# One place per operation in a planned order: attention and a gated MLP on one core

## The chip, the cores and the metric

The kernel runs on one core of a Trainium2 chip. The metric is the device time of one launch in microseconds. The engines are TensorE (PE, matmuls; its weight loads are listed as PEld), VectorE (DVE), ScalarE (ACT), GpSimd (POOL) and SyncE (SP, which issues most DMAs).

## The reference

```python
# attention: q, k, v of shape (4, 8, 576, 64)
q_rot, k_rot = (rotate(q), rotate(k))            # rotary embedding over halves of 64
scores = scale * np.matmul(q_rot, k_rot.transpose(0, 1, 3, 2))
scores = scores - np.max(scores, axis=-1, keepdims=True)
attn = np.exp(scores)
attn = attn / (np.sum(attn, axis=-1, keepdims=True) + 1e-09)
attn_out = np.matmul(attn, v)
# MLP over x = attn_out as (2304, 512), with w_in (512, 2048) and w_out (2048, 512)
h = x @ w_in
g = h * (1.0 / (1.0 + np.exp(-1.702 * h)))
return g @ w_out
```

## The kernel before, in words

**Tiling.** The 32 heads are worked on as 16 pairs. For a pair, `prep` (with `prep_qk`) loads q, k and v, applies the rotary embedding on POOL or DVE, and turns q and k with TensorE (L463). `scores` (L515) makes five blocks of scores; `softened` reduces each on DVE (L528), applies the exponential on ACT (L531), and for pairs 4 to 15 transposes 32x32 blocks on DVE (L536). `weighted` then forms the value product for pairs 4 to 15 in two halves of many small matmuls (L580); pairs 0 to 3 turn the weights on TensorE (L616) and use `weighted_whole`. `inverse_sums` brings the row sums through DRAM. The result is split into a high and a low part and written to `x_dram`.

**MLP.** Each product with float32 weights is made from such parts. `weight` loads one of 32 weight tiles (L710, into OW), converts it in nine steps on ACT (L714, L716), DVE (L718, L720, L723) and POOL (L726), and writes both parts into `win` or `wout`. `moe` works on chunks of 256 tokens: per block of 128 hidden columns twelve matmuls of the first layer into PT (L759), tanh on ACT (L765), a multiply on DVE that frees PT (L767), a split into G (ACT or POOL, then DVE or POOL), and six matmuls of the second layer (L776). The last four chunks are made by `two_chunks` with seven instead of eight products per pair of blocks; it needs sums of x (`sums`, tiles A and SX), made on DVE, and combinations of the weights (`differences`), which go through `t_dram`.

**What sets the order.** Every operation is given to a planner: `Plan.op` records it with its durations per engine it may run on, its dependences, its buffers, a priority and a release time. `Plan.run` plays the program through once as a list scheduler: whenever an engine is idle, it takes the ready operation with the lowest priority number whose buffers are free. For operations that two engines can do, the choice falls there too. The instructions are then issued in the order of the planned starts, so that each engine's queue has that order and runs it strictly, with waits on semaphores. In the kernel before, the priorities are times: tables for the pairs (PREP_AT, PAIR_AT, PAIR_LEN), the MLP (MOE_AT, MOE_STEP), the weights (WEIGHT_AT; WEIGHT_FROM is the release of their loads) and `differences` (T_AT), offsets in PLANNED, and NUDGE, which shifts 30 single operations.

Of the kernel before, what the change touches and what calls it, by code (L numbers as in the profile page):

```python
# [36 lines left out]
               -26154, 61379, -126384, 132121, -99291, -14531]  # L37
T_AT = [420394, -239827, 396523, 706563, 493117, 510553, 65805, 610849]
MORE_TIMES = ['T_AT']
NUDGE = {80: 7902, 153: 682, 235: 3974, 311: -1562, 313: -665, 315: 5307, 317: 1694, 320: 989, 394: -6842, 890:  # L40
         16599, 1142: -7665, 1171: 1126, 1181: -8648, 1199: -256, 1208: -44, 1252: 9550, 1943: -1091, 1953: 561,
         1955: 10337, 2043: 21717, 2131: 12833, 2217: 1319, 2236: -2623, 2245: -5223, 2316: -13089, 2610: 8963, 2746:
         819, 2970: 2878, 2976: 26303, 2977: 2097}
SLOTS = dict(SPS=3, PT=2, RAW=2, RAW1=1, BT=1, KP=2, ST=2, RT=3, XS=1, XC=4, T=1, G=1, O=2, OW=2, CW=2, TP=1, VR=1)
EARLY = dict(RAW=2, RAW1=1, BT=1, XS=1, KP=2, TP=1, VE=2, OW=3, CW=3)
ATTENTION = ("RAW", "RAW1", "BT", "KP", "ST", "RT", "XS", "TP", "VR")
# [5 lines left out]
PE, ACT, DVE, POOL, SP = "PE", "ACT", "DVE", "POOL", "SP"  # L52
# [25 lines left out]
class Plan:  # L78
# [23 lines left out]

    def op(self, durs, fn, deps=(), bufs=(), prio=0.0, moved=None, chain=None, columns=0.0,
           release=0.0, port=(), mode=("", ""), code=0.0):
        prio = prio + NUDGE.get(len(self.ops), 0.0)
        o = Op(len(self.ops), durs, fn, list(bufs), prio, moved, columns, release, port, mode, code)
        for d in {id(d): d for d in deps if d is not None}.values():
            d.out.append(o)
            o.before += 1
        if chain is not None:  # L110
            if chain in self.chains:
                self.chains[chain].then.append(o)
                o.before += 1
            self.chains[chain] = o
        for b in o.bufs:
            b.users.append(o)
        self.ops.append(o)
        return o
# [172 lines left out]
def attention_moe(ctx: ExitStack, tc: tile.TileContext, q, k, v, w_in, w_out, cos_sin, out):  # L291
# [69 lines left out]
    def dma(fn, nbytes, *deps, full=0, part=0, row=2048, land=900.0, by=SP, **kw):  # L361

        work, n = nbytes * (0.83 / row + 0.0032), full + part
        return op(by, 400.0 * full + 610.0 * part, fn, *deps,
                  moved=(work + 50.0 * n, work / n + 550.0, land + 300.0), **kw)
# [31 lines left out]
    def f():  # L397
        nc.vector.memset(plan.tiles["T"][0], 0.0)

    zeros = op(DVE, 140.0, f, prio=-1e6)  # L400
    warm = plan.buf("PT")
    for i in range(at["n_warm"]):
# [3 lines left out]
    def f():  # L406
        nc.gpsimd.memset(ident, 1.0)
        nc.gpsimd.affine_select(ident, ident, [[-1, 128]], compare_op=ALU.is_equal, fill=0.0, base=0,
                                channel_multiplier=1)

    constants = op(POOL, 1200.0, f, prio=-1e6)
    n_ve = early["VE"]

# [636 lines left out]
```

## Time and profile before

| What | us |
|---|---|
| median of 3 runs (690.1 to 691.67) | 690.37 |
| span of the profiled execution | 686.1 |
| the profiled execution's own total | not given beside the span |
| busy PE / PEld | 650.9 / 521.2 |
| busy DVE / ACT / POOL | 475.7 / 364.3 / 266.0 |

The span runs from the first to the last instruction of one profiled execution; the runs are timed without a profile. Busy times add up what the instructions of an engine cover, with the ends of pipelined matmuls modelled. Windows cut the span into stretches, the timeline shows instructions in order of time with the idle time just before them and what ended it, and the waits add such idle time by who waited for whom.

### The profile page before, as it was taken

The numbers are of one execution on the slowest core, as the hardware profiler recorded it, in microseconds if no ns is written. First come the engines' busy times: TensorE is split into PE (matmuls) and PEld (weight loads), VectorE is DVE, ScalarE is ACT, GpSimd is POOL, SyncE is SP. The second block draws the span as 40 slices with busy tenths as digits, with TensorE's granted clock in tenths as the row PEclk, the third lists the DMA queues.
The fourth block names the chain that finished last, engine by engine and source line by source line (L and its number), as shares of the span: only waits on it lengthen the run. The fifth ranks groups of instructions, "written<-read, shape, count | busy, mean of one in ns | idle before, by whom it ended". The sixth has DMA issues, their size and how long they took to land.

```text
span 686.1 us, 17932 instructions
## 1 busy us (share of the span) xinstructions
PE 650.9 (95%) x7160; PEld 521.2 (76%) x7160; DVE 475.7 (69%) x1041; ACT 364.3 (53%) x896; POOL 266.0 (39%) x269
## 2 busy tenths in 40 slices
PE   6899995999999999899999999999999999999997
PEld 4565554776778677767787878787989899998996
DVE  4999898899799889477847385728268445646342
ACT  2998985657676646254536253525235444533343
POOL 3766746635553567477663243111101000111000
PEclk8999999999999999999999999999999999999999
DMA  7965549668767556582737244143356223342111
GB/s 168 198 175 167 140 138 265 142 176 236 188 178 206 146 151 198 153 312 82 227 119 208 51 113 96 45 132 83 105 195 215 73 113 123 123 169 78 63 62 61
DMA packets 97539, 100.70 MB, mean 147 GB/s; under 512 B 61984, under 2 KB 81712, under 8 KB 93232
## 3 DMA queue, kind: packets, MB, share of 16 engines
q1 hardware_dynamic: 96400, 99.30, 50.0%
q8 instruction: 56, 0.92, 0.5%
q10 hardware_dynamic: 1056, 0.26, 0.2%
q14 instruction: 27, 0.22, 0.1%
HBM read 65.26 MB, written 23.67 MB: 130 GB/s over the span
## 4 chain that ended last, share of the span: by engine, by line
PE 71%; DVE 10%; DMA 8%; issue 4%; ACT 3%; POOL 2%; SPq 2%; POOLq 0%; DVEq 0%; ACTq 0%
PE SPS L941 13%; PE PT L759 13%; PE SPS L776 12%; PE SPS L515 9%; PE SPS L580 7%; PE PT L900 6%; PE SPS L900 6%; DMA OW<-in_moe_w_in_dram 2%; DVE TP L528 2%; DVE TP L536 2%; PE PT L616 2%; DMA OW<-in_moe_w_out_dram 2%; PE PT L463 2%; DMA RAW<-in_k_dram 2%; DMA RAW<-in_q_dram 1%
## 5 line engine op out<-in xcount | busy, mean ns | idle before, releaser
L759 PEld LDWEIGHTS PT<-XC,win 128*128 128x128 f32 x960 | 123.7, 190 | 23.7 <-DVE T L767 8.1
L759 PE MATMUL PT<-XC,win 128*128 128x256 f32 x960 | 134.3, 287 | 7.2 <-DVE T L767 4.5
L776 PE MATMUL SPS<-wout,G 128*128 128x512 f32 x480 | 131.8, 405 | 1.3 <-POOL G L359 1.3
L531 ACT ACTIVATE TP<-TP,ST 128x576 f32<-128x576 f32 x144 | 111.0, 773 | 33.7 <-DVE TP L528 33.1
L528 DVE TENSOR_SCALAR_CACHE_REDUCE TP<-SPS 128x576 f32<-128x576 f32 x144 | 103.8, 750 | 13.3 <-PE SPS L515 12.9
L515 PE MATMUL SPS<-KP 64*128 64x288 f32 (+1 forms) x640 | 103.5, 434 | 3.4 <-DVE TP L528 2.3
L776 PEld LDWEIGHTS SPS<-wout,G 128*128 128x128 f32 x480 | 83.7, 189 | 27.4 <-issue 6.9
L941 PE MATMUL SPS<-wout,G 128*128 128x512 f32 x384 | 93.0, 392 | 0.0
L359 DVE TENSOR_TENSOR G<-T,G 128x256 fp32r<-128x256 f32 x121 | 54.9, 463 | 50.8 <-ACT G L347 45.0
L536 DVE STREAM_TRANSPOSE TP<-TP 128x576 f32<-128x576 f32 x108 | 80.9, 765 | 10.4 <-ACT TP L531 10.0
L941 PEld LDWEIGHTS SPS<-wout,G 128*128 128x128 f32 x384 | 70.4, 188 | 13.9
L515 PEld LDWEIGHTS SPS<-KP 64*128 64x128 f32 (+1 forms) x640 | 54.3, 178 | 32.2 <-DVE TP L528 7.5
L347 ACT CAST G<-T 128x256 fp32r<-128x256 f32 x114 | 44.8, 405 | 63.6 <-PE SPS L776 46.1
L580 PE MATMUL SPS<-TP,VR 32*64 32x160 f32 (+1 forms) x3456 | 67.7, 293 | 9.1 <-issue 5.9
L580 PEld LDWEIGHTS SPS<-TP,VR 32*64 32x64 f32 x3456 | 59.2, 130 | 16.2 <-issue 10.7
L726 POOL TENSOR_TENSOR CW<-CW 128x512 int32<-128x512 int32 x32 | 42.8, 1339 | 62.1 <-DVE CW L723 17.7
L359 POOL TENSOR_TENSOR U<-U,U 128x256 f32<-128x256 f32 x16 | 12.0, 749 | 139.3 <-ACT U L347 109.0
L765 ACT ACTIVATE T<-PT 128x256 f32<-128x256 f32 x80 | 30.5, 381 | 49.9 <-PE PT L759 38.5
L767 DVE SCALAR_TENSOR_TENSOR T<-T,PT 128x256 f32<-128x256 f32 x80 | 33.1, 413 | 27.8 <-ACT T L765 27.2
L359 POOL TENSOR_TENSOR XS<-XS 128x576 fp32r<-128x576 f32 (+1 forms) x24 | 34.1, 1423 | 42.6 <-ACT XS L347 15.8
L350 POOL TENSOR_SCALAR G<-T 128x256 fp32r<-128x256 f32 x30 | 12.9, 428 | 77.5 <-PE SPS L776 37.8
L359 POOL TENSOR_TENSOR BT<-RAW,cos_sin_sb 128x512 f32<-128x512 f32 (+1 forms) x29 | 29.0, 1003 | 33.8 <-DMA RAW<-in_k_dram 12.9
(103 smaller groups left out, 936.9 us busy)
## 6 DMA issues: line engine op xcount, KB each, us to landing
TR<-t_dram SPq DMA_DIRECT2D x16, 1024.0 KB
VR<-VR SPq DMA_DIRECT2D x36, 288.0 KB
x_dram<-XS SPq DMA_DIRECT2D x16, 576.0 KB
XC<-x_dram SPq DMA_DIRECT2D x18, 512.0 KB
OW<-in_moe_w_in_dram SPq DMA_DIRECT2D x16, 512.0 KB
OW<-in_moe_w_out_dram SPq DMA_DIRECT2D x16, 512.0 KB
t_dram<-TS SPq DMA_DIRECT2D x8, 1024.0 KB
out_dram<-O SPq DMA_DIRECT2D x18, 256.0 KB
```

The source lines that it names most:

```text
L347: return nc.scalar.copy(to, src)
L359: return engine[e].tensor_tensor(to, a, b, op=how)
L515: nc.tensor.matmul(ss[h].t[:, c, 0:HALF] if t < 4 else ss[h].t[rows, c, 0:HALF], kq.t[rows, 1, t * 128:t * 128 + (128 if t < 4 else 64)], ...
L528: o = vec("DVE", "psum", S, lambda e: nc.vector.tensor_scalar(tp.t[:, t].rearrange("p (c s) -> p c s", c=2), s.t[:, :, 0:HALF], -1.0, LARG ...
L531: o = vec("ACT", "sbuf", S, lambda e: nc.scalar.activation(tp.t[:, t], tp.t[:, t], AF.Exp, bias=st.t[:, 0, t:t + 1], scale=-1.0, accum_out ...
L536: return o, vec("DVE", "psum", S, lambda e: nc.vector.transpose(tp.t[:, t], tp.t[:, t]), o, bufs=[tp], prio=prio + at["exp"] + at["across"])
L580: nc.tensor.matmul(bank[64 * h:64 * h + 64, to:to + 32 * (s1 - s0)], vr.t[rows, h, a], tp.t[rows, s0:s1, 32 * a:32 * a + 32], start=(a == ...
L726: o = vec("POOL", "two", DM, lambda e, a=a, r=r: nc.gpsimd.tensor_tensor(a().bitcast(I32), a().bitcast(I32), r(), op=ALU.add), o, low, buf ...
L759: nc.tensor.matmul(h.t[:, 0:CT], win[f_i // KH][:, wl, kk, f_i % KH * 128:(f_i % KH + 1) * 128], xc[xl].t[:, kk, :], start=(i == m == 0), ...
L776: nc.tensor.matmul(acc.t[:, m, :], g.t[:, a, m * 128:(m + 1) * 128], wout[f_i // KH][:, b, f_i % KH, :], start=(f_i == fs[0] and i == 0), ...
L900: nc.tensor.matmul(h(to), w(a)[:, k], x(b)[:, k], start=(begin and n == 0), stop=(n == 5), skip_group_check=True)
L941: nc.tensor.matmul(acc[j].t[:, m, :], g.t[:, x, m * 128:(m + 1) * 128], wout[f_i // KH][:, y, f_i % KH, :], start=(begin and n == 0), stop ...
```

## The change

Each operation gets a place of its own, by its number in the order in which the code creates the operations. The place takes the part of the priority; the release comes from HELD where the number stands in it and is 0 elsewhere; a letter in ENGINES would leave an operation one engine only. NUDGE is gone. The tables of times are still in the code, but for each of the 2998 operations the place overrides them. HELD has 16 numbers, all of them loads of weights; ENGINES has 2998 dots. No operation, dependence or buffer is changed.

```diff
-NUDGE = {80: 7902, 153: 682, 235: 3974, 311: -1562, 313: -665, 315: 5307, 317: 1694, 320: 989, 394: -6842, 890:
...
+PLACES = [2, 0, 10, 18, 11, 8, 17, 15, 19, 6, 12, 16, 14, 3, 1, 7, 5, 21, 22, 24, 27, 31, 9, 28, 32, 35, 38, 42, 41,
...
+          2984, 2986, 2988, 2989, 2996, 2997]
+HELD = {1161: 61703, 1170: 33528, 1197: 49667, 1206: 107335, 1215: 94361, 1224: 0, 1251: 58829, 1296: 97830, 1305:
+        101045, 1323: 8666, 1332: 92779, 1341: 156202, 1359: 91161, 1377: 1324, 1395: 60303, 1413: 114354}
+ENGINES = ("...................................................................................................."
...
-        prio = prio + NUDGE.get(len(self.ops), 0.0)
+        n = len(self.ops)
+        if n < len(PLACES):
+            prio, release = PLACES[n], HELD.get(n, 0.0)
+            if ENGINES[n] != ".":
+                e = {"A": ACT, "V": DVE, "G": POOL}[ENGINES[n]]
+                durs = {e: durs[e]}
```

## Rows read from the trace of the kernel before

**Rows 1.** Windows: from:to and length, busy us of each engine, PEclk, DMA, GB/s
```profile
0.00:20.00 20.00, 13.10 (x70) 9.84 (x70) 11.32 (x24) 6.99 (x16) 8.39 (x17) 0.83 0.78 174
20.00:100.00 80.00, 75.29 (x571) 45.65 (x569) 73.87 (x165) 72.98 (x173) 53.11 (x46) 1.00 0.63 167
100.00:124.00 24.00, 16.31 (x349) 11.78 (x348) 19.10 (x39) 12.69 (x33) 12.78 (x10) 0.93 0.70 195
124.00:340.00 216.00, 206.19 (x2790) 162.55 (x2790) 180.73 (x376) 127.00 (x305) 126.14 (x120) 1.00 0.67 189
340.00:500.00 160.00, 158.80 (x2263) 128.59 (x2263) 92.28 (x207) 67.36 (x173) 48.32 (x52) 1.00 0.39 109
500.00:512.00 12.00, 10.75 (x68) 9.37 (x67) 8.05 (x17) 3.92 (x9) 0.00 (x0) 1.00 0.34 126
512.00:676.00 164.00, 164.00 (x1036) 148.55 (x1035) 89.13 (x217) 70.25 (x186) 17.25 (x26) 1.00 0.32 112
676.00:686.10 10.10, 6.47 (x28) 4.90 (x27) 1.25 (x4) 3.10 (x7) 0.00 (x0) 1.00 0.27 104
```

**Rows 2.** Chain that ended last, 478 to 515 us: start, us, what
```profile
496.53 1.43 PE PT L759 x12
...
505.58 3.09 DVE A L359 x5
```

**Rows 3.** Timeline of PE, 100 to 124 us: start, us, instruction, [idle before, releaser]
```profile
108.65 2.73 PE L580 MATMUL SPS<-TP,VR 32*64 32x160 f32 x144 [2.92 <-DVE TP L536]
...
114.34 2.40 PE L580 MATMUL SPS<-TP,VR 32*64 32x128 f32 x118 [2.07 <-issue]
...
120.26 0.58 PE L759 MATMUL PT<-XC,win 128*128 128x256 f32 x2 [2.15 <-issue]
```

**Rows 4.** Timeline of ACT and PE around 150 and 232 us
```profile
149.98 0.70 ACT L714 ACTIVATE CW<-OW 128x512 int32<-128x512 uint32 x1 [2.47 <-DMA OW<-in_moe_w_in_dram]
...
153.57 1.09 PE L759 MATMUL PT<-XC,win 128*128 128x256 f32 x7 [1.26 <-DVE T L767]
...
232.05 0.66 ACT L714 ACTIVATE CW<-OW 128x512 int32<-128x512 uint32 x1 [2.38 <-DMA OW<-in_moe_w_out_dram]
...
233.49 1.22 PE L759 MATMUL PT<-XC,win 128*128 128x256 f32 x8 [1.25 <-DVE T L767]
```

**Rows 5.** Timeline of SP's queue: the loads that ACT waited for in rows 4
```profile
143.68 0.54 SPq L710 DMA_DIRECT2D OW<-in_moe_w_in_dram  x1
...
224.92 1.35 SPq L710 DMA_DIRECT2D OW<-in_moe_w_out_dram  x1
```

**Rows 6.** Waits of ACT for weight loads, whole span: total us, times, longest
```profile
ACT CW L714 <- DMA OW<-in_moe_w_out_dram: 5.9, 4, 2.4
...
ACT CW L714 <- DMA OW<-in_moe_w_in_dram: 4.3, 3, 2.5
```

**Rows 7.** Waits of PE, 124 to 340 us: total us, times, longest
```profile
PE SPS L580 <- issue: 3.5, 5, 1.6
PE PT L759 <- DVE T L767: 2.9, 3, 1.3
PE SPS L776 <- POOL G L359: 1.3, 2, 1.1
PE PT L549 <- ACT KP L354: 0.9, 1, 0.9
```

**Rows 8.** Timeline of PE: second halves of products of pairs 6, 7 and 9
```profile
178.01 1.59 PE L580 MATMUL SPS<-TP,VR 32*64 32x128 f32 x74 [0.91 <-issue]
...
214.95 2.73 PE L580 MATMUL SPS<-TP,VR 32*64 32x160 f32 x144
...
279.69 0.79 PE L580 MATMUL SPS<-TP,VR 32*64 32x128 f32 x28 [1.57 <-issue]
```

**Rows 9.** One line's instructions on DVE (ns min/median/max), and a group of the page
```profile
L718 DVE TENSOR_SCALAR CW<-CW x32: 379/428/1518, 19.0 to 241.5; 128x512 f32<-128x512 f32 x32
...
L528 DVE TENSOR_SCALAR_CACHE_REDUCE TP<-SPS 128x576 f32<-128x576 f32 x144 | 103.8, 750 | 13.3 <-PE SPS L515 12.9
```

More of the change, by code (lines that the diff above doesn't have):

```diff
@@ L39 @@
 MORE_TIMES = ['T_AT']
-NUDGE = {80: 7902, 153: 682, 235: 3974, 311: -1562, 313: -665, 315: 5307, 317: 1694, 320: 989, 394: -6842, 890:
-         16599, 1142: -7665, 1171: 1126, 1181: -8648, 1199: -256, 1208: -44, 1252: 9550, 1943: -1091, 1953: 561,
-         1955: 10337, 2043: 21717, 2131: 12833, 2217: 1319, 2236: -2623, 2245: -5223, 2316: -13089, 2610: 8963, 2746:
-         819, 2970: 2878, 2976: 26303, 2977: 2097}
+PLACES = [2, 0, 10, 18, 11, 8, 17, 15, 19, 6, 12, 16, 14, 3, 1, 7, 5, 21, 22, 24, 27, 31, 9, 28, 32, 35, 38, 42, 41,
[157 rows of a table added]
@@ new lines @@
+HELD = {1161: 61703, 1170: 33528, 1197: 49667, 1206: 107335, 1215: 94361, 1224: 0, 1251: 58829, 1296: 97830, 1305:
+        101045, 1323: 8666, 1332: 92779, 1341: 156202, 1359: 91161, 1377: 1324, 1395: 60303, 1413: 114354}
+ENGINES = ("...................................................................................................."
+           "...................................................................................................."
+           "...................................................................................................."
+           "...................................................................................................."
+           "...................................................................................................."
+           "...................................................................................................."
+           "...................................................................................................."
+           "...................................................................................................."
+           "...................................................................................................."
+           "...................................................................................................."
+           "...................................................................................................."
+           "...................................................................................................."
+           "...................................................................................................."
+           "...................................................................................................."
+           "...................................................................................................."
+           "...................................................................................................."
+           "...................................................................................................."
+           "...................................................................................................."
+           "...................................................................................................."
+           "...................................................................................................."
+           "...................................................................................................."
+           "...................................................................................................."
+           "...................................................................................................."
+           "...................................................................................................."
+           "...................................................................................................."
+           "...................................................................................................."
+           "...................................................................................................."
+           "...................................................................................................."
+           "...................................................................................................."
+           "..................................................................................................")
```

156 rows, old and new, of the table PLACES are left out of this document.

## The prediction, made before the changed kernel had run

> **What bounds the kernel now.** I read the windows first, then what TensorE waits for, then the timeline around the largest gaps, then the chain of waits. The windows [rows 1] show TensorE (PE) as the bound: it is busy 650.91 of 686.10 us, so 35.19 us are idle, and these lie in this way: 0 to 20 us 6.90; 20 to 100, where only attention runs, 4.71; 100 to 124, 7.69; 124 to 340, where attention and the MLP are mixed and the late weights come in, 9.81; 340 to 500, 1.20; 500 to 512, at the change to the last four chunks, 1.25; 512 to 676 nothing; the tail 3.63. VectorE (DVE) is close behind PE until 340 us (73.87 of 80 us, then 180.73 of 216) and has room after that (92.28 of 160). No operation is added, removed or moved to a given engine, so PE's own work stays; the change can only win idle time, and PE time in which a matmul stands behind its weights and is counted as busy.
>
> **How I read the new order.** The list PLACES is a permutation of 0 to 2997, and no operation stands in it before one whose result it needs. It can be read as the order itself, apart from operations that the plan finds not ready. Beside it I put the order of the kernel before, operation by operation, and measured the distances in PE work, with durations like the 1.43 us of twelve first-layer matmuls [rows 2]. ENGINES holds dots only, so it forces nothing; HELD only holds loads back in the plan and issues nothing. Of the 872 PE operations 756 have another position, but the first 17 us of PE work keep theirs, nearly all. Pairs 4 to 9 begin their scores between 5 us of PE work earlier and 5 later; pairs 10 and 11 some 11 earlier, pairs 12 to 15 17 to 21 earlier, and MLP blocks move back in exchange. The end of attention is thus some 20 us further from the last chunks.
>
> **The change, stretch by stretch.**
>
> *0 to 20 and the tail (10.53 us idle).* Nearly the same sequence at both ends: 0, between -0.5 and +0.5.
>
> *20 to 100.* DVE has 6.1 us idle here and is what PE waits for. In front of the first value product of pair 4 the new list puts two more weight operations on DVE, about 1.2 us of work. Cover is DVE's idle time; without it PE starts that product up to 1.2 us later. In exchange the scores of pairs 1 to 3 are spaced more evenly. I take 0, between -1.5 and +1.2.
>
> *100 to 124.* Three gaps: 2.92 us until the last transposes of pair 4, then 2.07 and 2.15 us of "issue", in the second half of that product and behind it [rows 3]. The new list keeps score, turn, product, sums, product, first layer in this sequence with only 0.3 us more turn work in the first gap. -0.3, between -2 and +1.2.
>
> *124 to 340, the late weights.* Two of the larger gaps have one cause: ScalarE (ACT) stands 2.47 and 2.38 us before a weight that has not landed, the tanh behind it in ACT's queue is late, DVE's multiply frees PT late, and PE stands 1.26 and 1.25 us [rows 4]. These loads were issued 6.30 and 7.13 us before that use (143.68 to 149.98 and 224.92 to 232.05) [rows 4, 5]. In PE work, the orders put 4.1 and 5.7 us between load and first use. Taking 6.3 us as the time that a load wants, I add up by how much the 32 distances fall short: before, 21.0 us in the early sixteen and 25.0 in the late sixteen; in the new list 10.6 and 19.0. The shortest distances grow from 1.4 and 1.5 us to 2.7 and 3.0. That is a third less in all and a quarter less among the late ones. ACT's wait for weights is 10.2 us now [rows 6]; a quarter off the 2.51 us of PE gaps is -0.6, and since the loads also spread, I take -1.0, between -2.5 (all gone) and +2.5 (two more such gaps: three late loads, f8 and f10 of w_out and f15 of w_in, are now used after only 3.0 to 3.5 us, and the load that cost the second gap after 4.3 instead of 5.7).
>
> *124 to 340, the halves of a value product.* PE stands 3.5 us at "issue" in L580 [rows 7]. Two of these gaps, 0.91 and 1.57, fall in pairs 6 and 9, whose two halves follow each other directly; where other matmuls lie between, as for pair 7, the second half starts without a gap [rows 8]. The new list puts 3.0 and 2.1 us of other work between the halves of pairs 6 and 9, but leaves only 0.2 us at pair 7 and 1.2 at pair 13. -2.5 for the two, +1.5 for the new ones: -1.0, between -2.5 and +1.5.
>
> *124 to 340, the rest.* The turn of pair 8's sums, late by 0.9 us behind ACT [rows 7], is moved behind both halves of the product: -0.9. The second layer that stands 1.1 us behind GpSimd's G (1.3 in all) [rows 7] gets other neighbours: -0.6, between -1.3 and +1.
>
> *340 to 512.* Nothing in the first part: 1.20 us idle, 0. At 505.58 DVE makes five sums for the last chunks in a row, 3.09 us [rows 2]; the multiply that frees PT stands behind them, and PE waits 1.25 us in the stretch to 512 [rows 1]. In the new list the ten sums start 6.7 us of PE work after their loads and lie one by one between the multiplies: -1.05, between -1.25 and +2. The upper end is DVE standing at its head for a load: the distance was 9.4 us. What should hide it is that in the list these loads go ahead of both t_dram loads on SP's queue; before, one of the two went first.
>
> *Stalls that PE's busy time hides.* With fewer late landings and no bunched multiplies some go too: -1.2, between -5 and +2. No row shows them alone; I take a value near zero because the rows with idle time shrink by half only.
>
> **Sum.** 0 + 0 - 0.3 - 1.0 - 1.0 - 0.9 - 0.6 - 1.05 - 1.2 = -6.05 us: a span of 680.05. The profiled execution has a span of 686.1, and its own total is not given beside it; the median of the runs, 690.37, is 4.3 above, which I leave as it is. So 684.3; I say 684.5.
>
> **Rivals.**
> 1. *Much better:* the idle time from 124 to 512 goes altogether, 12.3 us: 678.1. For it speaks that PE has no gap from 512 to 676 with the same kinds of blocks; against it that four of the causes above remain in the new list in other places. Chance 0.14.
> 2. *No change:* the gaps that vanish come back at the next thing that is late (the softmax chain of the pair that was pulled ahead, or short load distances as listed above), or too many operations were not ready at their place and the plan's order comes out near the old one. 690.4, within 1.4. About 0.2%, 1.4 us, is what runs of this kernel can tell from no change. Chance 0.14.
> 3. *Slower:* DVE becomes late between 200 and 400 us. A pair's nine reductions and nine transposes take some 0.75 us each on DVE [rows 9], 13.5 us; three quarters of a pair pulled ahead are 10 us, less about a third for the MLP blocks that move back: some 7 us more in front of the same PE point near 340 us, 188 of 216 us. That alone fits. But a DVE operation that overlaps GpSimd's takes far longer than its median: 1518 ns against 428 for L718 [rows 9], 1.1 us, as much as the cover that a multiply has before PE stands. If one such stretch meets a multiply in each of the eight pairs from 6 to 13, PE stands eight times 1.25 us [rows 4], +10 us on the forecast: 694.5. Five of them use up the gain and from seven on it is plainly slower; seven give +8.75, 693.2, and that is my price. Against it: the plan lets GpSimd begin only after the last DVE operation that it knows to collide. The Trainium skill ("SBUF — State Buffer", "Who interferes with whom") says that VectorE and GpSimd take their common port pair as an exclusive lock, and that whichever issues first makes the other wait; by that rule, an order that brings GpSimd's rope beside other DVE work can pay whole instructions; eight such meetings would give the 694.5 above, and the spread of L718 agrees with the rule. Chance 0.19.
>
> **Chances and range.** The forecast has 0.53. Faster by over 0.2%: forecast and rival 1, 0.67; within: 0.14; slower: 0.19. The forecast's own range, its terms' ends not taken all at once, is 680.5 to 688. The whole range must take in most of rivals 1 and 2 and the milder part of 3: 678.5 to 692.5.
>
> **What would show it.** PE's idle time from 124 to 340 near 6 us instead of 9.8, and 0.2 instead of 1.25 around the last chunks; ACT's wait for OW near 7 us; no "issue" gap between the halves of pairs 6 and 9, but one at pair 7; the three gaps from 108 to 121 still there; PE's busy time 650 within 2. Wrong it would be if PE's gaps behind DVE's L767 became more than five, if the sums waited for A at DVE's head, or if the gaps from 100 to 124 changed by more than 2 us, since I see nothing in the order that touches them.

## The result, and the profile after

The changed kernel takes 682.49 us (median of 4 runs, 677.96 to 684.56); the kernel before, beside it, 690.45 (690.1 to 691.67). The ratio is 0.9875, 95% interval 0.9841 to 0.991: 8.0 us faster, well clear of the noise. The forecast was 684.5 in a range of 678.5 to 692.5. The profiled execution took 681.47 us, its span 679.4.

The same windows as [rows 1], of the kernel after; only the last one ends earlier:

```profile
0.00:20.00 20.00, 13.91 (x58) 10.41 (x60) 10.19 (x22) 6.52 (x14) 8.32 (x17) 0.75 0.78 171
20.00:100.00 80.00, 76.64 (x584) 47.22 (x582) 76.12 (x185) 74.03 (x173) 48.13 (x42) 1.00 0.61 171
100.00:124.00 24.00, 16.43 (x363) 11.88 (x360) 20.68 (x40) 11.64 (x30) 12.76 (x11) 1.00 0.72 197
124.00:340.00 216.00, 210.44 (x3066) 166.88 (x3065) 186.06 (x402) 127.17 (x308) 124.44 (x118) 0.98 0.68 192
340.00:500.00 160.00, 158.19 (x2007) 130.51 (x2006) 90.05 (x199) 66.12 (x167) 50.01 (x54) 1.00 0.39 112
500.00:512.00 12.00, 12.00 (x86) 11.22 (x85) 2.96 (x8) 4.67 (x12) 0.73 (x1) 1.00 0.62 208
512.00:676.00 164.00, 163.82 (x1011) 146.51 (x1009) 84.32 (x210) 70.64 (x189) 12.40 (x18) 1.00 0.29 102
676.00:679.40 3.40, 0.00 (x0) 0.00 (x0) 0.00 (x0) 0.50 (x1) 0.00 (x0) 0.95 0.20 77
```

The window's length minus PE's busy time (the number behind the length) gives PE's idle time. Before and after: 6.90 and 6.09, 4.71 and 3.36, 7.69 and 7.57, **9.81 and 5.56**, 1.20 and 1.81, 1.25 and 0, 0 and 0.18, 3.63 and 3.40. Together 35.19 and 27.96. PE's busy time went from 650.91 to 651.44, so the span is shorter by 7.23 - 0.53 = 6.70 us. More than half of that lies in 124 to 340. The 2.16 us from 0 to 100 are not the order's: over all traces of the runs below, PE's idle time there is 9.3 to 11.6 us with the old order and 9.4 to 11.0 with the new one. In 124 to 340 the two orders stay apart: 9.81, 13.98 and 12.12 us in the traces that have the old order there unchanged (before, b_sums, h_ab129), 5.56, 5.59 and 7.27 with the new one (the kernel after twice, h_ba129). The trace of before is the best of its three, so the pair compared here shows the stage's gain too small.

What PE waited for there, against [rows 7], and what is left of ScalarE's waits for weight loads over the whole span, against [rows 6] (total us, times, longest):

```profile
PE SPS L771 <- issue: 5.1, 2, 2.7
PE PT L950 <- DVE T L958: 0.4, 1, 0.4
...
ACT CW L905 <- DMA OW<-in_moe_w_out_dram: 0.5, 1, 0.5
```

L771, L950, L958 and L905 are L580, L759, L767 and L714 of before. In the window before, PE waited 6.1 us for results of other engines (the rows of that view sum to 2.9 for T, 1.3 for G and 1.9 for KP and TP). Now it waits 0.4. ScalarE's wait for weights fell from 11.0 us (the two rows and a third of 0.8) to 0.5. Only the "issue" time grew, from 3.7 to 5.1. It stands in two places, and a third large gap lies ahead of them (timeline of PE: start, length, what, idle time ahead of it):

```profile
117.38 0.86 PE L950 MATMUL PT<-XC,win 128*128 128x256 f32 x5 [3.11 <-DMA XC<-x_dram]
...
143.72 0.53 PE L771 MATMUL SPS<-TP,VR 32*64 32x128 f32 x3 [2.73 <-issue]
...
214.90 1.06 PE L771 MATMUL SPS<-TP,VR 32*64 32x160 f32 x23 [2.32 <-issue]
```

The first is the first token chunk, which is loaded 3.4 us later than before. The second is the end of pair 5's first half, the third pair 7's second half. Such a stall can cost more than its length. Windows around the two (third number from the end: granted clock; the next: share of the DMA engines that is busy):

```profile
142.00:146.00 4.00, 2.28 (x9) 1.46 (x9) 1.83 (x3) 0.84 (x3) 0.52 (x1) 0.64 0.39 124
146.00:150.00 4.00, 4.00 (x17) 3.70 (x16) 2.25 (x6) 2.90 (x6) 0.00 (x0) 0.50 0.36 82
150.00:152.00 2.00, 2.00 (x94) 1.86 (x99) 2.00 (x6) 0.77 (x2) 0.76 (x1) 1.00 0.23 12
...
214.00:216.00 2.00, 1.10 (x33) 1.08 (x33) 1.36 (x3) 0.00 (x0) 0.51 (x1) 0.71 0.13 45
216.00:219.00 3.00, 3.00 (x25) 2.40 (x15) 0.00 (x0) 1.05 (x4) 2.03 (x2) 0.63 0.49 110
```

After each, PE runs for some us at the lower of its two levels (0.50, 1.2 GHz), and this time counts as busy.

### The profile page after: what moved, and what is told of

The parts are those of the page before. It is cut to its first block, busy times and chain, and to the rows that moved or that the text cites. A ratio compares the mean times of both kernels' runs of the same rounds, so it can differ in the third digit from the quotient of the medians.

```text
span 679.4 us, 17933 instructions
## 1 busy us (share of the span) xinstructions
PE 651.4 (96%) x7160; PEld 524.6 (77%) x7160; DVE 470.4 (69%) x1060; ACT 361.3 (53%) x889; POOL 256.8 (38%) x257
## 4 chain that ended last, share of the span: by engine, by line
PE 87%; ACT 5%; DVE 3%; issue 3%; DMA 1%; POOL 1%; DVEq 0%; POOLq 0%; ACTq 0%; SPq 0%
PE PT L950 17%; PE SPS L967 16%; PE SPS L1132 13%; PE SPS L706 12%; PE SPS L771 9%; PE SPS L1091 6%; PE PT L1091 6%; PE PT L654 2%; PE PT L807 2%; PE SPS L831 2%; ACT TP L722 1%; ACT TP L538 1%; PE PT L594 1%; DVE TP L727 1%; DMA XC<-x_dram 1%
## 5 line engine op out<-in xcount | busy, mean ns | idle before, releaser
L950 PEld LDWEIGHTS PT<-XC,win 128*128 128x128 f32 x960 | 125.9, 191 | 25.7 <-issue 8.9
L950 PE MATMUL PT<-XC,win 128*128 128x256 f32 x960 | 138.2, 290 | 5.3 <-DMA XC<-x_dram 3.1
L706 PE MATMUL SPS<-KP 64*128 64x288 f32 (+1 forms) x640 | 101.3, 435 | 2.4 <-DVE TP L719 1.8
L727 DVE STREAM_TRANSPOSE TP<-TP 128x576 f32<-128x576 f32 x108 | 82.5, 772 | 12.8 <-ACT TP L722 12.5
L550 DVE TENSOR_TENSOR G<-T,G 128x256 fp32r<-128x256 f32 x114 | 50.3, 445 | 41.5 <-ACT G L538 38.7
L538 ACT CAST G<-T 128x256 fp32r<-128x256 f32 x116 | 46.6, 405 | 56.7 <-PE SPS L967 26.9
L771 PE MATMUL SPS<-TP,VR 32*64 32x160 f32 (+1 forms) x3456 | 68.4, 295 | 7.0 <-issue 5.5
L771 PEld LDWEIGHTS SPS<-TP,VR 32*64 32x64 f32 x3456 | 59.7, 131 | 13.9 <-issue 9.2
L958 DVE SCALAR_TENSOR_TENSOR T<-T,PT 128x256 f32<-128x256 f32 x80 | 32.5, 407 | 29.4 <-ACT T L956 29.0
L550 POOL TENSOR_TENSOR XS<-XS 128x576 f32<-128x576 f32 (+1 forms) x26 | 37.1, 1425 | 28.1 <-DVE G L550 22.8
L541 POOL TENSOR_SCALAR G<-T 128x256 fp32r<-128x256 f32 x28 | 11.6, 414 | 79.6 <-PE SPS L1132 25.8
L1121 ACT ACTIVATE T<-U 128x256 f32<-128x256 f32 x64 | 25.7, 417 | 25.8 <-DVE U L550 24.1
```

The lines of the kernel that those rows point to most:

```text
L538: return nc.scalar.copy(to, src)
L550: return engine[e].tensor_tensor(to, a, b, op=how)
L706: nc.tensor.matmul(ss[h].t[:, c, 0:HALF] if t < 4 else ss[h].t[rows, c, 0:HALF], kq.t[rows, 1, t * 128:t * 128 + (128 if t < 4 else 64)], ...
L727: return o, vec("DVE", "psum", S, lambda e: nc.vector.transpose(tp.t[:, t], tp.t[:, t]), o, bufs=[tp], prio=prio + at["exp"] + at["across"])
L771: nc.tensor.matmul(bank[64 * h:64 * h + 64, to:to + 32 * (s1 - s0)], vr.t[rows, h, a], tp.t[rows, s0:s1, 32 * a:32 * a + 32], start=(a == ...
L950: nc.tensor.matmul(h.t[:, 0:CT], win[f_i // KH][:, wl, kk, f_i % KH * 128:(f_i % KH + 1) * 128], xc[xl].t[:, kk, :], start=(i == m == 0), ...
```

## The experiments

Two questions were open. Where does the gain come from, and is it what the prediction's terms say? And what are the "issue" stalls: two adjoining halves that use up instructions too fast (my reason, here theory A), or data transfers that stand ahead of the instructions (theory B)? That instructions come by DMA is in the page of each kernel: a queue of kind "instruction" with 56 packets and 0.92 MB, 16.4 KB each.

Each run's name stands in its heading. Kernels whose name begins with b_ start from before and have its line numbers, those with a_ start from after; the two h_ kernels (hybrids) have the order of one up to 128 us and of the other from there. The a_ and b_ kernels keep the plan and move a few operations in the order that it gives out; operations are named by their number in the plan:

```diff
-        for o in plan.order():
+        for o in moved(plan.order()):
+def moved(order):
+    for at, some in MOVES:          # the operations `some` go just ahead of operation `at`
+        ops = [o for i in some for o in order if o.idx == i]
+        order = [o for o in order if o.idx not in some]
+        k = next(j for j, o in enumerate(order) if o.idx == at)
+        order[k:k] = ops
+    return order
```

Runs of one chip are compared with each other. On the first chip: after_again, a_split7, a_dma7, a_fill; on the second: the three b_ kernels and a_ow5; the last four ran together.

**The changed kernel again (after_again).** 

> The changed kernel once more, beside the others of this chip. Both theories: median 681 to 684 us against 690.4 of before, runs spread over some 5 us. The three stalls of TensorE that are put down to issue (2.73 us in pair 5's value product at 143.72, 2.32 us in pair 7's second half at 214.90, 1.34 us at 105.73) come back at the same places within 0.5 us, and so does the 3.11 us wait for the first token chunk's load at 117.38. If the stalls move from execution to execution, neither theory of them holds and they are the cause of the spread.

679.04 us (676.94 to 682.41) against 689.28; ratio 0.985 (0.9815 to 0.9884). The stalls came back in their places, 2.40 us at 143.58, 1.39 at 212.98, 1.35 at 105.47, and 2.03 for the chunk; pair 7's and the chunk's were 0.9 and 1.1 us shorter, outside the 0.5 expected: the places are fixed, the sizes are not. Between the shortest and the longest of these six runs the clock can account for the difference: the span of 675.1 had a mean granted clock of 0.987, that of 680.5 had 0.979. As an estimate from these figures, (1 - 0.987) x 675.1 = 8.8 and (1 - 0.979) x 680.5 = 14.3 us of full-speed time are lost; the difference is 5.5 us, the spans differ by 5.4. In general it does not: two of the four runs of the result had 0.982 both, and spans of 676.1 and 681.6.

**Halves of pair 7 parted (a_split7).**
```diff
+MOVES = [(594, [1607, 1608, 1609, 1605, 1606]), (595, [1610]), (747, [1611])]
```


> The changed kernel with the two halves of pair 7's value product parted by a block of the MLP (its first layer and the second layer of the block before, 18 matmuls, 3.4 us of work that stood behind the second half). Theory A, adjacency: two halves of 144 small matmuls back to back use up the instructions faster than they are brought; parted, the 2.32 us stall at 214.90 goes, and with it the half clock of 216 to 219: 3 to 4 us less than the changed kernel. Theory B, crowding: the instructions come late because data transfers of 204 to 212 stand ahead of them; the second half starts 3.4 us later but the transfers are the same, so a stall of 1 us or more stays somewhere between 208 and 218 and the kernel gains less than 1.5 us.

677.53 us (676.19 to 680.17): not told apart from the changed kernel. PE's timeline:

```profile
209.91 1.84 PE L771 MATMUL SPS<-TP,VR 32*64 32x160 f32 x91
212.60 1.31 PE L771 MATMUL SPS<-TP,VR 32*64 32x128 f32 x53 [0.85 <-issue]
214.63 1.47 PE L706 MATMUL SPS<-KP 64*128 64x288 f32 x8 [0.72 <-ACT XS L538]
...
217.72 0.51 PE L706 MATMUL SPS<-KP 64*128 64x288 f32 x2 [0.95 <-DVE TP L719]
```

The stall between the halves went, one of 0.85 us came inside the second half, and the MLP block taken from behind it had covered the copy out of the product (0.72) and the maxima (0.95). There is no half clock at 216 to 219, but after_again, on the same chip, has none there either, so that is not this edit's doing. Theory A alone would have left no stall; theory B had asked for 1 us or more.

**Transfers of pair 7 postponed (a_dma7).**
```diff
+MOVES = [(1347, [1593]), (1593, [1404]), (1404, [757])]   # all behind 602
```


> The changed kernel with the halves of pair 7 left back to back, but four of SyncE's transfers (a load of key blocks at 207.47, a weight load at 209.39, two partial results at 208.84 and 209.87) issued only behind the small transfer that went out at 210.84. Theory B, crowding: with the transfer share of 206 to 212 falling from 0.9 to below 0.6 the stall at 214.90 falls from 2.32 us to below 0.8, 2 to 3 us less in the whole. Theory A, adjacency: the stall stays above 1.4 us (the uncrowded stall of the kernel before, in pair 9, was 1.57 us), and the whole stays within 1.5 us of the changed kernel, worse where the postponed loads are waited for.

675.26 us (674.37 to 678.45); ratio to before 0.9796 (0.9762 to 0.9831). The transfer share of 206 to 212 fell from 0.89 in after_again to 0.59, and the stall, with the halves still back to back:

```profile
207.35 0.28 PE L740 MATMUL PT<-ident,ST 128*9 128x128 f32 x1
207.56 2.12 PE L771 MATMUL SPS<-TP,VR 32*64 32x160 f32 x109
210.06 1.03 PE L771 MATMUL SPS<-TP,VR 32*64 32x160 f32 x35 [0.39 <-issue]
```

0.39 us instead of 1.39. That speaks for theory B, and other runs agree: with these transfers in place this stall was 2.32, 1.39, 1.21 (a_fill) and 2.87 us (a_ow5), with them postponed 0.39, 0.66 (a_dma57) and 0.50 (a_all). The medians lie 3.8 us apart, the profiled spans (672.7 and 675.1) 2.4: of these, 1.85 are PE's idle time in 124 to 340 (3.74 against 5.59) and 1.5 lie in 0 to 100, where the two kernels do the same in the same order, so not all of the distance is the edit's.

**The first chunk's wait filled (a_fill).**
```diff
+MOVES = [(1222, [393, 392, 391, 394]), (1442, [489, 425]), (1223, [429, 426])]
```


> The changed kernel with work drawn into the wait for the first token chunk (3.11 us at 117.38): ScalarE copies pair 4's value products out ahead of a weight cast that stood waiting for GpSimd until 117.59, and TensorE takes four transposes and the first scores of pair 5 (some 2 us of work) ahead of the first MLP block. If the gain of the change is idle time of TensorE taken out and nothing else, the same must hold here: the wait falls to about 1.0 us, the 0.94 us wait for pair 5's first maxima at 121.99 goes, and the kernel is 2 to 3 us faster than the changed one. The rival: the stage of 124 to 340 is bound by VectorE (186 of 216 us busy) or by the late weights, and what is won by 124 is waited away before 340; then the whole stays within 1 us.

678.19 us (676.84 to 684.89), not told apart from after_again; the 2 to 3 us did not come. The waits of 2.03 and 0.96 us went; these came:

```profile
116.62 0.75 PE L706 MATMUL SPS<-KP 64*128 64x288 f32 x3 [0.34 <-ACT XS L538]
...
124.75 0.50 PE L967 MATMUL SPS<-wout,G 128*128 128x512 f32 x1 [1.82 <-ACT G L538]
126.27 1.04 PE L967 MATMUL SPS<-wout,G 128*128 128x512 f32 x3 [0.78 <-POOL G L550]
```

The rival was right in its result; the new wait is for the first block's casts, behind weight work in the queues of ACT and POOL.

**The two halves' term by itself, in the kernel before (b_split69).**
```diff
+MOVES = [(526, [1538, 1539, 1540, 1535, 1536, 1537]), (527, [1541]), (1310, [1542]),
+         (730, [1723, 1724, 1725, 1721, 1722]), (2206, [1726, 1727])]
```


> The kernel before with the adjoining halves of the value products of pairs 6 and 9 parted, each by five MLP operations that stood behind the second half, and nothing else. Theory A, adjacency: the stalls of 0.91 us at 178.01 and 1.57 us at 279.69 go; minus 2 to 3 us, the two halves' term of the prediction. Theory B, as the two kernels with pair 7 left it: the stall follows the transfers that run beside the second half (share 0.37 to 0.74 here) and the work taken from behind the half no longer covers the copy out of the products and the next scores' maxima; the stalls shrink to some 0.5 us, new waits of 0.7 and 0.9 us stand behind each second half, and the whole moves by less than 1 us.

691.68 against 690.81 us, ratio 1.0022 (1.0 to 1.0043). No stall is left in pairs 6 and 9, although the transfer share in the 2 us before the instruction packet that each second half runs into was 0.75 and 0.79 here, against 0.61 and 0.87 in before: parting the halves is enough for these, as theory A says. The 2.5 us did not come out at the end. Behind the parted halves stand:

```profile
181.91 1.00 PE L515 MATMUL SPS<-KP 64*128 64x288 f32 x4 [0.63 <-ACT XS L347]
...
186.43 0.96 PE L776 MATMUL SPS<-wout,G 128*128 128x512 f32 x3 [0.72 <-DVE G L359]
188.58 0.62 PE L759 MATMUL PT<-XC,win 128*128 128x256 f32 x3 [0.52 <-DVE T L767]
...
289.21 0.96 PE L776 MATMUL SPS<-wout,G 128*128 128x512 f32 x3 [1.67 <-DVE G L359]
```

**The late weights by themselves (b_late).**
```diff
+MOVES = [(463, [614]), (636, [628]), (612, [560])]
```


> The kernel before with three transfers (key blocks at 142.5, value rows of two pairs at 184 and 223) put behind the weight loads that stood behind them (143.68, 187.12, 224.92). By the prediction's term for late weights: ScalarE's waits of 5.9 and 4.3 us for these loads shrink to some 3 us each, and the waits of 1.26 and 1.25 us at 153.57 and 233.49, which I put down to weight work that came in late and held VectorE, go: minus 1 to 2.5 us. The rival: those two waits of TensorE are one chunk's own latency (last scores, multiplication, cast) with nothing late in it; then ScalarE waits less and the whole stays within 0.5 us.

691.79 us, ratio 1.002 (0.9997 to 1.0043). The term's mechanism is there in part: ScalarE's waits for w_out fell from 5.9 to 2.6 us (those for w_in rose from 4.3 to 5.7), PE's wait for T in 124 to 340 fell from 2.9 to 0.7, the one at 233.49 is gone and the one at 153.57 is 0.72. The gain in time is not there: a cast of GpSimd took its place 6 us further on. PE and POOL there:

```profile
240.23 0.97 PE L776 MATMUL SPS<-wout,G 128*128 128x512 f32 x3 [2.67 <-POOL G L359]
...
236.88 1.27 POOL L359 TENSOR_TENSOR BT<-RAW,cos_sin_sb 128x512 f32<-128x512 f32 x1 [4.65 <-DVE TP L536]
238.23 1.26 POOL L359 TENSOR_TENSOR RAW<-RAW,cos_sin_sb 128x512 f32<-128x512 f32 x1
239.45 0.72 POOL L359 TENSOR_TENSOR G<-T,G 128x256 fp32r<-128x256 f32 x1
```

G stood in POOL's queue behind two rope operations, the first of which waited 4.65 us for VectorE.

**The five sums by themselves (b_sums).**
```diff
+MOVES = [(2289, [2188])]
```


> The kernel before with one multiplication of VectorE (chunk 14 of the last token chunk) ahead of the third of five sums instead of behind the fifth. By the prediction's term: the 1.25 us wait of TensorE at 509.06 goes, the sums end 0.4 us later, and the kernel is 1.0 to 1.25 us faster. The rival: the stage behind begins with products of these sums and waits as much longer; then nothing moves.

690.16 us, ratio 0.9992 (0.9969 to 1.0014). The 1.25 us before the last block (here 511.05) went, and 0.40 + 0.62 + 0.24 = 1.26 came:

```profile
511.05 1.59 PE L759 MATMUL PT<-XC,win 128*128 128x256 f32 x12
513.04 0.73 PE L776 MATMUL SPS<-wout,G 128*128 128x512 f32 x2 [0.40 <-ACT G L347]
514.40 1.19 PE L776 MATMUL SPS<-wout,G 128*128 128x512 f32 x4 [0.62 <-DVE G L359]
...
516.54 0.74 PE L900 MATMUL PT<-SX,TR 128*128 128x256 f32 x4 [0.24 <-DVE T L767]
```

**Pair 5's transfers postponed (a_ow5).**
```diff
+MOVES = [(551, [1368]), (1368, [1296])]
```


> The changed kernel with the two weight loads of 137.33 issued only behind the load of key blocks that goes out at 144.96. Pair 5's first half stands alone between other work, and yet its last five matmuls came after a stall of 2.73, 2.4, 1.5, 1.9 and 2.0 us in the runs so far, each behind a transfer share above 1.0 at 136 to 138. Theory B, crowding: with the share below 0.6 there the stall falls below 0.8 us, and the half clock of 144 to 150 that follows it in some runs goes with it: 2 to 4 us in the whole, and less spread between executions, unless the two late loads are waited for. Theory A, adjacency, gives no reason for this stall and none for it to go: it stays above 1.5 us.

681.98 us against 690.81, ratio 0.988 (0.9846 to 0.9913): nothing won over the changed kernel's own ratios. At 136 to 138, where the expectation looked, the share was still 1.00 (1.06 in after_again). What fell is the share from 138 on: in steps of 2 us 0.50, 0.00 and 0.05, against 0.76, 0.40 and 0.80. And the stall, with what followed:

```profile
141.97 0.49 PE L771 MATMUL SPS<-TP,VR 32*64 32x128 f32 x5 [0.35 <-issue]
150.63 0.70 PE L967 MATMUL SPS<-wout,G 128*128 128x512 f32 x1 [2.00 <-ACT G L538]
155.55 0.76 PE L706 MATMUL SPS<-KP 64*128 64x288 f32 x4 [1.24 <-ACT XS L538]
```

Theory B holds for this stall: the same matmuls, 0.35 instead of 2.40 us. The trace shows the step between: the instruction packet before the stall went out at 139.61, when PE had begun 1126 of its matmuls; in after_again it went out at 141.36, after 1225. The postponed loads were then waited for (4.6 us by ScalarE), which cost PE the 2.00 and 1.24 us above, and pair 7's stall was 2.87 us in this run, with half clock after it.

**Old beginning, new order from 128 us on (h_ba129).**
```diff
-PLACES = [...]; HELD = {...}; ENGINES = ("...")     # those of the change
+# t[op]: start in the plan before for its first 610 operations, in the plan after (moved to the joint) for the rest
+PLACES = ranks of t;  HELD = {op: t[op] - 0.01};  ENGINES = the engine that each had there
```


> The kernel before up to the second token block of the MLP's first chunk (some 128 us: the first 610 of 2998 operations), and from there the order of the changed kernel, engine by engine (of the 746 operations that TensorE has left, two stand otherwise than there). If the gain lies in 124 to 340, where TensorE's waits for other engines' results sum to 5 to 9 us in the four traces with the order of before and to 1 us or less in those of the changed kernel, this kernel keeps most of it: these waits below 2 us, the whole 6 to 9 us below before. The rival, that the first 128 us are what counts (pair 4, the first MLP chunk and the weights come earlier there, and what follows inherits it): within 2 us of before.

680.45 us (678.15 to 683.51) against 690.59: ratio 0.9852 (0.9829 to 0.9874), the whole gain of the change. Waits of PE in 124 to 340:

```profile
PE SPS L771 <- issue: 4.6, 3, 2.5
PE PT L950 <- issue: 1.4, 1, 1.4
PE SPS L967 <- POOL G L550: 0.4, 1, 0.4
PE SPS L706 <- ACT XS L538: 0.3, 1, 0.3
PE PT L950 <- DVE T L958: 0.3, 1, 0.3
```

**New beginning, old order from 128 us on (h_ab129).** The same edit the other way round, with 625 operations. 

> The counterpart: the changed kernel's first 625 operations (up to 128 us) and then exactly the order of before on every engine. If the gain lies behind 124 us: the waits of 124 to 340 sum to 5 to 9 us as before, and the whole is 0 to 3 us below before, the idle time that the first stages lost (35.2 - 28.0 us in all, of which 2.3 before 124). The rival, the first 128 us: 6 us or more below before.

689.29 us (687.33 to 692.45): ratio 0.998 (0.9966 to 0.9995). Waits of PE in 124 to 340, and ScalarE's for weights over the span:

```profile
PE PT L950 <- DVE T L958: 3.3, 4, 1.9
PE SPS L771 <- issue: 2.5, 2, 2.0
PE SPS L967 <- POOL G L550: 2.0, 1, 2.0
PE SPS L706 <- DVE TP L719: 2.0, 2, 1.3
...
ACT CW L905 <- DMA OW<-in_moe_w_out_dram: 7.2, 5, 3.1
ACT CW L905 <- DMA OW<-in_moe_w_in_dram: 4.1, 4, 1.9
```

The two make the cut clean: the place is what changed behind 128 us, and with it PE's waits for results (1.0 us with the new order, 8.5 with the old). That is more than the order of each queue. The new places also led the plan to other choices where two engines can do an operation: of 708 such operations that both hybrids have behind the joint, 190 are on another engine. No run parts order from choice of engine.

**Two combinations (a_dma57 and a_all).**
```diff
+MOVES = [(1347, [1593]), (1593, [1404]), (1404, [757]), (551, [1368])]          # a_dma57
+# a_all: the same, and
+         (1222, [393, 392, 391, 394]), (1442, [489, 425]), (1223, [429, 426]),
+         (1445, [430]), (1276, [427, 1446, 1447]), (1212, [1448])
```


> The changed kernel with the postponed transfers of pair 7 (which gave 675.3 against 679.0 us) and, of pair 5's two weight loads of 137.33, one alone put behind the load of key blocks that follows; both put back took pair 5's stall from 2.4 to 0.35 us, but ScalarE then waited for them and TensorE with it, 2.0 and 1.2 us. Theory B, crowding: with one load less the stall is 0.5 to 1.5 us, no wait of 1 us or more stands at 148 to 156, and the kernel is 1 to 2 us below the one with pair 7's transfers alone (-14 us against before there), so 14 to 17 us below before. If half the crowding is as bad as the whole, the stall stays near 2 us and nothing is won.

678.67 us (677.38 to 680.78), ratio 0.9832 (0.9812 to 0.9852): 11.9 us below before, not 14. The stalls were 1.56 us in pair 5 and 0.66 in pair 7. Half the crowding is not told apart from the whole: with both loads in place pair 5's stall was 1.51 to 2.73 us in five traces.

> The same with the work drawn into the first chunk's wait as well (copies out of pair 4's products ahead of a weight cast, four transposes and a score block ahead of the first MLP block); there the wait of 2.0 us for the chunk's load and 0.95 us for maxima went, but 1.8 and 0.8 us for the first block's casts came, since ScalarE and GpSimd had weight work ahead of them. Now those casts stand ahead of that work too. If each wait is paid by the queue that holds it: waits of 116 to 128 below 1.5 us in sum and 1 to 2 us below the other kernel of this pair, so 15 to 19 us below before. If the stage is bound by VectorE: no difference from it.

679.46 us (678.45 to 680.45), ratio 0.9841 (0.9824 to 0.9857). From 112 to 130 us PE's waits fell from 2.43 + 0.96 us to 0.35 + 0.47 + 1.42 + 0.40, and further on one of 2.17 us stood at 174.18 before the transposes of a later pair. The waits of 116 to 128 sum to 2.3 us, not to below 1.5, and the time is not told apart from a_dma57's.

The lowest time measured is that of a_dma7: 675.26 us beside 679.04 of the changed kernel and 689.28 of before on its chip. Its own runs and those of the changed kernel overlap by 1.5 us, and the two kernels built on it, on another chip, did not go lower in their ratios, so I call it ahead of before, and likely but not surely ahead of the changed kernel.

## Why the prediction was right, and where it was not

The time and its sign were right: 684.5 forecast, 682.49 measured; -6.05 forecast for the span, -6.70 in the profiled runs. The place was right too. Its largest sum lay in 124 to 340 (-3.5; measured -4.25), and the two hybrids show that what changed behind 128 us, the order with the engine choices that came with it, carries the gain. The parts of that sum were not right, and that the total came out so close is partly luck. Against the forecast, "issue" time in 124 to 340 came out 2.4 us worse and PE's busy time 1.7, while PE's waits for results there went by 5.7 us where 2.5 had been forecast, and 0 to 100 was 2.2 us better by the chance of one execution.

- **Late weights, -1.0: too small.** This was the part that moved. ScalarE's wait for loads was forecast at 7 us and came out at 0.5 (2.3 in the second profile), and PE's waits for T in the stretch went from 2.9 to 0.4. The failing step was "taking 6.3 us as the time that a load wants": in the kernel after, a load issued at 173.83 was first used at 177.90 after a wait of 0.52, so it wanted 4.07 us, and one issued at 150.94 was used at 154.91 without a wait. The trace of before had shown as much: the seven loads behind 124 us that were waited for took 3.72 (172.09 to 175.81) to 7.13 us, and 6.3 is near the upper end. Nor is it a fixed time: in after_again two loads were waited for until 4.65 and 4.86 us after their issue. The 6.3 and 7.1 of [rows 4, 5] held the transfers ahead of the load; b_late, which took some of them away, brought these two waits down to 1.39 and 0.17 us. In the kernel after, the sixteen late loads were used 3.97 to 11.8 us after their issue, and one was waited for. Counted by 6.3, the new list's distances looked only a third better.
- **Halves of the value products, -1.0: wrong sign.** Pairs 6 and 9 lost their gaps and pair 7 got one, as said (in after_again pair 9 has one of 0.64). But issue time in the stretch rose by 1.4 us, through 2.32 us in pair 7 (1.5 was the price for new ones) and 2.73 us in pair 5, which I did not look for, since its halves are apart. The step that failed is the cause: adjoining halves are one cause, as b_split69 shows; the data transfers ahead of the instructions are another, and in pairs 5 and 7 the larger: 2.40 to 0.35 and 1.39 to 0.39 us when transfers alone were postponed.
- **Pair 8's sums -0.9, GpSimd's G -0.6:** both waits of [rows 7] went. Here the forecast held.
- **Five sums in a row, -1.05:** the gap of 500 to 512 went to zero and did not come back in the next window (0.18). The cause was right, but the cure is not the one multiplication: moved alone, it took the wait away and gave nothing in time. The new order spreads all ten sums.
- **Hidden stalls, -1.2:** PE's busy time rose by 0.5 in the first profile and fell by 2.0 (to 648.9) in that of after_again. Time at half clock counts as busy, so neither shows the term: it stays open.
- **100 to 124, -0.3:** -0.1 in sum, but by exchange: the gaps of 2.92, 2.07 and 2.15 us became 1.34, 1.54, 0.46 and 3.11 (the chunk's load). So one gap went by over 2 us and one of 3.11 came: by the sign that the prediction itself named, its reading that nothing in the order touches these gaps was wrong.
- **20 to 100, 0:** -1.35 in this pair of traces, inside its bounds, but no more than executions differ (4.7 us of idle time here in before, 3.4 in h_ba129, with the same order).
- **From span to median:** I put the median 4.3 us above the span. Only about 2 of these lie outside the span (681.47 and 679.4 here); the rest is that the profiled run of before was a quick one. To keep the 4.3 was still right, since the forecast is of a median: from median to median the change was -8.0, against -6.05. With 2.07 us in place of 4.3 the same sum gives 682.1, nearer to 682.49 only because it would set a quick run against a typical one.

Rival 3 (VectorE late by its port) is out: PE's waits for T fell to 0.4 us though VectorE did more in the stretch, 186.06 against 180.73 us busy. Rival 2, gaps that vanish and come back at the next thing late, is what every single repair in the old order showed (1.0022, 1.002, 0.9992), and a_fill and a_ow5 in the new one. It is not what the change showed. My reading, which no run tests, is that the change moves all queues at once, while a repair cures a wait on one engine and leaves the queue of the next in the old order.

What stays open: which of the some 2370 places behind 128 us matter, and how much is due to the engines that the plan chose anew. Cuts further in were not tried. That the waits vanish together, and that each of three single repairs in the old order wins nothing, is shown; that fewer places than all would do is not excluded.

## What to carry to other kernels

Here a sum of gaps came near what a new order as a whole won, with misses in its terms that cancelled, and it was a poor forecast of what a single repair wins: ask for each cured wait which queue stands next, and look 5 to 10 us further on in the trace. Before using issue-to-use as the time of a load, see what was ahead of it in the queue. Where TensorE stalls at "issue" in a run of many small matmuls, look how long transfers run on ahead of the instruction packet that ends the stall, and try to move transfers as well as matmuls. Neither is free: a_ow5's loads were then waited for, and behind b_split69's parted halves other waits came.

## What the runs showed of the hardware that I had not expected

- TensorE's instructions share the DMA engines with data. Of the same runs of small matmuls, those of pairs 5 and 7 stalled for 1.39 to 2.73 us in the two traces of the changed kernel, and for 0.35 and 0.39 where transfers had been moved away. The queue's 56 packets for 7160 matmuls and 7160 weight loads make some 256 a packet (an estimate that takes the queue to be TensorE's), fewer than the 144 matmuls and 144 weight loads of a half. A half takes 2.73 us, so a packet lasts some 2.4 us there. In pair 5's stalls of 2.73, 2.40 and 0.35 us and in the one of 1.57 us below, TensorE went on 2.2 to 2.4 us after a packet's start: in such a run a packet that starts late is felt at once. The Trainium skill ("Trainium Architecture — The Big Picture", "The software stack") has instructions of 64 bytes. By that figure one of the packets of 16.4 KB holds an estimated 256 of them, which agrees.
- The packet goes out as the transfers ahead of it thin out. Pair 9 of before stalled 1.57 us until 279.69 [rows 8]; over 276 to 278 the share is 0.61, which looks harmless, but it was 1.00 shortly before the packet, which went out at 277.41 (the second number from the end is the share):

```profile
275.40:276.90 1.50, 1.22 (x80) 1.22 (x86) 0.17 (x1) 0.00 (x0) 1.08 (x1) 1.00 1.00 415
276.90:277.40 0.50, 0.50 (x45) 0.50 (x38) 0.28 (x1) 0.00 (x0) 0.19 (x1) 1.00 0.48 180
277.40:279.40 2.00, 0.72 (x40) 0.42 (x23) 1.44 (x3) 0.00 (x0) 1.08 (x1) 1.00 0.04 12
```

- The same in pair 5: in the kernel after, the share was 0.80 from 139.5 to 140.5, 0.06 from 141.0 to 141.5, and the packet went out at 141.51; in a_ow5 it was 1.05 from 137.5 to 138.5, 0.00 from 139.0 to 139.6, and the packet went out at 139.61. Pair 7's packet in after_again went out amid the transfers (share 1.16 just before) and took 1.86 us, in a_dma7 (share 0.35) 0.93.
- A stall that long can be paid twice: after the two of the kernel after, the granted clock was 0.50 (1.2 GHz) from some 143 to 150 and 0.63 on average from 216 to 219. After the one of 1.39 us in after_again, it stayed at 1.00 from 212 to 218. So the same kernel can pay or not pay for it; how much of the spread between executions this makes is open, as the two spans with a mean clock of 0.982 show.
